# Attention with beacon keys and a squared-ReLU MLP: v of batches 0 and 1 cast in the transfer, chunk 1's second product by seven half-size products, second loads that wait for q, and a new order of work

## The chip, the cores and the metric

The kernel runs on one core of a Trainium2 chip. The metric is device time in microseconds (us) of one execution. Three runs of the kernel before took 327.59, 330.63 and 332.34 us, a median of 330.63. A core has TensorE (PE in the profile), VectorE (DVE), ScalarE (ACT), GpSimd (POOL) and SyncE (SP); DMA transfers are issued from the queues of SP, ACT and POOL, and only those that POOL issues change the data type on the way in this kernel.

## The reference

Eight batches, eight heads, 576 tokens, head size 64, and 16 "beacon" keys and values ahead of each head's own. Everything goes in and out in fp32.

```python
scores = matmul(q, concat([beacon_k, k]).T) / sqrt(64)      # causal over k; beacons are always seen
a = softmax(scores)
x = matmul(a, concat([beacon_v, v]))                        # -> x [4608 tokens, 512]
h = x @ w_in                                                # w_in  [512, 2048]
g = relu(h) ** 2
out = g @ w_out                                             # w_out [2048, 512]
```

## The kernel before

**Tiling.** Attention goes by batch and by pair of heads (four pairs p per batch, numbered on: batch b has pairs 4b to 4b+3). For a pair, scores are made with keys on the partitions (`qk` words, L695 in batch 0, L688 after it) into one of two PSUM strips, exponentiated by ACT into `pt` (`exp` words, L717 and L800), masked on the diagonal by a product with `tri` on DVE (`mask`, L823), multiplied with the 65-column tiles `vb` (v and a column of ones, so that the row sum comes along; `av`, L845), and normalised by DVE into `xn` (`norm`, L862 and L864). `xn` is transposed into `xT`, by TensorE in batches 0 to 2 (`xtp`, L913; evacuated by `xte` words on ACT or DVE) and by DMA from SP's queue after them (`xt`, L896).

The MLP goes by nine chunks j of 512 tokens. The first product is 16 groups of four 128x128x512 matmuls (`s1.j.f`, L1147), each evacuated through a relu (`relu`, ACT L1162 or DVE L1164) into `g` and squared in place, two groups at a time (`sq`, ACT L1172 or DVE L1174). Groups of chunk 0 are cut in a part 0 and a part 1, as batch 0 and batch 1 deliver its tokens. The second product has two forms. For j < FAST (chunks 0 and 1) it is plain: for each of four 128-token tiles, 16 matmuls 512 wide (`s2.j.ts.qd`, L1197) and one evacuation `ev`. For the other chunks it is done with seven products of half the size in place of eight: four sums of `g` in two parts on DVE (`sumj.n.i`, L1228), sums of `w_out` made once (`wsum`, L956), 14 groups of eight 256-wide matmuls (`s2.j.n.t`, L1256), and seven evacuations that add the products up in `osb` (`ev`, copies at L350 or L352 and adds at L1279). The first product of chunks 7 and 8 is also done with seven products (`h` words, L1024). A chunk's result goes out from `osb` by SP (`st`, L1185).

**Loads.** Batch 0's first part of q and k comes in fp32 into `osb` (`fldk`, `fldq`, L589: q of the first two pairs on ACT's queue, the others on SP's) and is cast by DVE or ACT (`fc`). Its second part (`sld0k1`, `sld0q1`) and batch 1's q and k (`sld1...`) come cast, by POOL's queue (L513), and are transposed by TensorE (`two`, `tp`, `ek`, `eq`). v comes by `add_load` in five tiles of up to 128 rows, eight heads and 64 columns: in batches 0 and 1 by POOL's queue, later by SP's, in fp32 into one of six slots `stg`, and from there a copy casts it into `vb` (`cast`, on POOL, at L352; two casts of batch 0 on DVE). `vb` has 65 columns per head, so a run of v in it is 128 bytes. `w_in` comes in four quarters by POOL's queue (`win0`, `win2`, `win1`, `win3`, L937), cast on the way, and so does `w_out` (`wout`, L945). From batch 2 on k comes by SP's queue into `stg` and q by POOL's (`ldq`), both are put into bf16 (`cast`, `join`) and transposed by DMA on SP (`tr`, L471).

**Order.** The list `SEQUENCE` is written out by hand: `Order.run` (L184) issues one operation for each word, in this order, so it fixes the order on every engine and every queue; a letter behind `@` picks the engine (A is ACT, D is DVE, P is POOL). Slots of `stg`, `ps` (four PSUM banks) and the strips are taken and given back in the same order. Where an operation has `sync`, each transfer that it issues waits for the transfer named there. `add_part_loads` has the parameter, and nothing gives it one.

## Time and profile before

| | before |
|---|---|
| three runs, us | 332.34, 327.59, 330.63 |
| profiled execution, us | 327.58 |
| its span, us | 325.8 |
| granted TensorE clock, mean | 0.998 |
| TensorE busy | 311.4 us, 96% |
| VectorE / ScalarE / GpSimd busy | 235.2 / 222.9 / 100.0 us |
| moved by DMA | 48.43 MB, mean 149 GB/s |

The span runs from the first to the last instruction of the profiled execution; the 1.8 us between it and that execution's time lie around it. TensorE has almost all of the span, so the questions are what its work takes, and where it waits. A row of a timeline has start, length, engine, line, operation, out<-in and count, and in brackets the idle time before it and what ended that. Letters and line numbers are those of the kernel before.

### The profile page before, as it was taken

The numbers are of one execution on the slowest core, as the hardware profiler recorded it, in microseconds if no ns is written. First come the engines' busy times: TensorE is split into PE (matmuls) and PEld (weight loads), VectorE is DVE, ScalarE is ACT, GpSimd is POOL, SyncE is SP. The second block draws the span as 40 slices with busy tenths as digits, with TensorE's granted clock in tenths as the row PEclk, the third lists the DMA queues.
The fourth block names the chain that finished last, engine by engine and source line by source line (L and its number), as shares of the span: only waits on it lengthen the run. The fifth ranks groups of instructions, "written<-read, shape, count | busy, mean of one in ns | idle before, by whom it ended". The sixth has DMA issues, their size and how long they took to land.

```text
span 325.8 us, 8454 instructions
## 1 busy us (share of the span) xinstructions
PE 311.4 (96%) x3440; PEld 226.1 (69%) x3460; DVE 235.2 (72%) x512; ACT 222.9 (68%) x333; POOL 100.0 (31%) x157
## 2 busy tenths in 40 slices
PE   2899899999999999999989999999999999999995
PEld 1579664644555468888776478655788788888884
DVE  3895985625545799666986687657968498989882
ACT  3996986378846897876755876648982664886810
POOL 9954852246610425240762114205000310000000
PEclk9999999999999999999999999999999999999999
DMA  7999999999994999898999995994500600030033
GB/s 156 213 204 210 201 206 174 175 181 258 200 161 115 224 222 179 126 193 168 262 152 164 199 221 139 178 206 117 127 14 9 179 19 2 0 132 0 2 147 113
DMA packets 127103, 48.43 MB, mean 149 GB/s; under 512 B 107864, under 2 KB 122072, under 8 KB 127064
## 3 DMA queue, kind: packets, MB, share of 16 engines
q1 hardware_dynamic: 108298, 35.48, 51.2%
q0 software_dynamic: 18112, 12.03, 25.3%
q8 instruction: 27, 0.44, 0.6%
q10 hardware_dynamic: 654, 0.38, 0.4%
q14 instruction: 12, 0.10, 0.1%
HBM read 37.22 MB, written 9.44 MB: 143 GB/s over the span
## 4 chain that ended last, share of the span: by engine, by line
PE 86%; DVE 5%; ACT 5%; DMA 1%; issue 1%; SPq 1%; ACTq 0%; DVEq 0%
PE ps L1147 27%; PE ps L1256 23%; PE ps L845 9%; PE ps L1197 8%; PE strip L1024 4%; PE strip L688 4%; PE ps L1024 3%; PE strip L1256 2%; PE ps L688 2%; PE strip L695 2%; DVE g L1174 2%; ACT pt L800 1%; DMA osb<-in_k_dram 1%; DVE pt L823 1%; PE ps L913 1%
## 5 line engine op out<-in xcount | busy, mean ns | idle before, releaser
L1147 PE MATMUL ps<-xT,w_in 128*128 128x512 bf16 (+6 forms) x626 | 103.4, 314 | 1.8 <-DVE g L1164 0.9
L1147 PEld LDWEIGHTS <-w_in 128*128 128x128 bf16 x640 | 57.4, 98 | 37.2 <-issue 2.9
L800 ACT ACTIVATE pt<-strip 128x1024 bf16<-128x1024 f32 (+3 forms) x77 | 70.4, 956 | 8.2 <-PE strip L688 4.6
L1162 ACT ACTIVATE g<-ps 128x512 bf16<-128x512 f32 (+2 forms) x80 | 42.4, 550 | 30.5 <-PE ps L1147 24.8
L1256 PEld LDWEIGHTS <-g 128*128 128x128 bf16 x448 | 42.5, 98 | 7.6 <-issue 1.9
L352 POOL CAST vb<-stg 128x512 bf16<-128x512 f32 (+1 forms) x38 | 25.9, 710 | 69.3 <-DMA stg<-in_v_dram 57.7
L823 DVE TENSOR_TENSOR pt<-pt,tri 128x512 bf16<-128x512 bf16 (+1 forms) x93 | 35.4, 404 | 13.2 <-ACT pt L800 12.9
L1164 DVE TENSOR_SCALAR g<-ps 128x512 bf16<-128x512 f32 (+2 forms) x48 | 29.0, 610 | 17.9 <-PE ps L1147 12.3
L845 PEld LDWEIGHTS <-pt 128*128 128x128 bf16 x930 | 34.8, 100 | 7.0 <-issue 0.9
L1256 PE MATMUL ps<-w_out,g 128*128 128x256 bf16 x304 | 38.3, 273 | 0.2 <-DVE xn L864 0.2
L845 PE MATMUL ps<-vb,pt 128*128 128x65 bf16 x930 | 37.4, 195 | 0.1
L1256 PEld LDWEIGHTS <-sum_area 128*128 128x128 bf16 x336 | 32.0, 98 | 5.4 <-issue 1.4
L864 DVE TENSOR_TENSOR xn<-ps,rcp 128x320 bf16<-128x320 f32 (+2 forms) x64 | 31.5, 492 | 2.2
L350 ACT COPY osb<-ps 128x512 f32<-128x512 f32 x24 | 14.0, 586 | 24.9 <-PE ps L1256 20.6
L352 POOL CAST qk_area<-stg 128x512 bf16<-128x512 f32 (+1 forms) x30 | 19.1, 657 | 38.3 <-DMA stg<-in_k_dram 38.0
L1172 ACT ACTIVATE g<-g 128x1024 bf16<-128x1024 bf16 (+2 forms) x32 | 29.6, 939 | 1.8 <-DVE g L1164 1.0
L1197 PE MATMUL ps<-w_out,g 128*128 128x512 bf16 x122 | 30.1, 379 | 0.3
L800 ACT ACTIVATE pt<-ps 128x512 bf16<-128x512 f32 x42 | 23.9, 601 | 8.8 <-PE ps L688 6.7
L1174 DVE TENSOR_TENSOR g<-g 128x1024 bf16<-128x1024 bf16 (+2 forms) x32 | 21.3, 681 | 9.3 <-ACT g L1162 9.2
L1256 PE MATMUL ps<-w_sum,sum_area 128*128 128x256 bf16 x208 | 27.0, 273 | 1.0 <-DVE osb L1279 1.0
L862 DVE RECIPROCAL rcp<-ps 128x5 f32<-128x5 f32 (+2 forms) x64 | 12.1, 189 | 12.8 <-PE ps L845 11.1
L688 PEld LDWEIGHTS <-kT 64*128 64x128 bf16 x432 | 13.9, 96 | 9.7 <-issue 7.4
(106 smaller groups left out, 407.5 us busy)
## 6 DMA issues: line engine op xcount, KB each, us to landing
out_dram<-osb SPq DMA_DIRECT2D x16, 512.0 KB, 3.4
stg<-in_k_dram SPq DMA_DIRECT2D x18, 256.0 KB, 4.5
stg<-in_v_dram SPq DMA_DIRECT2D x18, 256.0 KB, 4.9
stg<-in_q_dram POOLq DMA_DIRECT2D x12, 256.0 KB, 5.6
w_in<-in_moe_w_in_dram POOLq DMA_DIRECT2D x4, 512.0 KB, 11.7
w_out<-in_moe_w_out_dram POOLq DMA_DIRECT2D x4, 512.0 KB, 11.8
stg<-in_v_dram POOLq DMA_DIRECT2D x6, 256.0 KB, 8.6
stg<-in_k_dram SPq DMA_DIRECT2D x6, 224.0 KB, 4.3
```

What stands on the lines that cost most here:

```text
L352: eng[e].tensor_copy(dst, src)
L688: nc.tensor.matmul(out, kT[b % 2][hp, pr, 128 * c:128 * c + 128], rhs, start=True, stop=True)
L800: nc.scalar.activation(out, in_, AF.Exp, bias=0.0, scale=scale)
L823: nc.vector.tensor_tensor(out=d, in0=d, in1=tri[0:rows, m0:m0 + m, 0:w][:, None].to_broadcast([rows, 2, m, w]), op=ALU.min)
L845: nc.tensor.matmul(a[0:w, at + (t - tl[0]) * (D + 1):at + (t - tl[0] + 1) * (D + 1)], P[0:rr, hj, o:o + w], vb[b % 2][0:rr, c, 2 * pr + hj ...
L864: nc.vector.tensor_tensor(out=xn[b % 2].rearrange("p t (h d) -> p h t d", d=D)[:, h0:h0 + nh, tl[0]:tl[0] + nt], in0=a[:, :, :, 0:D], in1= ...
L1147: nc.tensor.matmul(h[:, lo - spans[0][0]:hi - spans[0][0]], w_in_sb[:, mc, ft * 128:(ft + 1) * 128], xT[:, mc, lo % RING:lo % RING + hi - lo],
L1162: nc.scalar.activation(dst, h, AF.Relu, bias=0.0, scale=1.0)
L1164: nc.vector.tensor_scalar(out=dst, in0=h, scalar1=0.0, scalar2=None, op0=ALU.max)
L1172: nc.scalar.activation(d, d, AF.Square, bias=0.0, scale=1.0)
L1197: nc.tensor.matmul(o, G[:, fc, ts * 128:(ts + 1) * 128], w_out_sb[:, fc, :], start=(fc == 0), stop=(fc == NFT - 1))
L1256: nc.tensor.matmul(o, lhs[:, f, t * 128:(t + 1) * 128], rhs[:, f], start=fresh and f == 0, stop=f == HF - 1, skip_group_check=True)
```

## The change

It has four parts.

1. v of batches 0 and 1 is written by the transfer straight into `vb` in bf16: no `stg` slot, no cast, the ten `cast0v` and `cast1v` words go. The transfers are on POOL's queue as before. Later batches' v is as before.
2. `FAST` goes from 2 to 1: chunk 1's second product is done by the seven half-size products. That adds eight `sum1` words and has 14 groups of eight for 16 of four, and seven evacuations for four.
3. The first transfer of batch 0's second part (`sld0k1.0`) waits for the transfer of the first q (`fldq0`).
4. `SEQUENCE` is written anew throughout: 1,532 words for 1,533, with the order changed in all batches and many engine letters too (relu on ACT 79 for 88, squares on ACT 48 for 43, joins on POOL fewer).

```diff
-    FAST = 2
+    FAST = 1
...
         soft = b <= 1
-        queue = nc.gpsimd if soft else nc.sync
+
+        if soft:
+            def emit_direct(e):
+                dst = vb[b % 2][:, c, :, 0:D]
+                insts = []
+                if lo:
+                    insts.append(nc.gpsimd.dma_start(out=dst[0:Nb], in_=beacon[b].transpose([1, 0, 2])))
+                insts.append(nc.gpsimd.dma_start(out=dst[lo:rows],
+                                                 in_=t[b, :, t0:t0 + rows - lo, :].transpose([1, 0, 2])))
+                return insts
+
+            ld = add(f"ld{b}{x}{c}", "POOL", 1.35 if lo else 0.9, emit_direct,
+                     dma=1.0 * rows / 128, behind=load_chain[-1:] + behind, sync=sync)
+            load_chain.append(ld)
+            cast[b, x, c] = ld
+            return
...
-        engs = ("POOL", "DVE") if b == 0 and c <= 1 else ("POOL",)
-        cast[b, x, c] = add(f"cast{b}{x}{c}", engs, {"DVE": 0.42, "POOL": 0.63}, emit_cast,
+        cast[b, x, c] = add(f"cast{b}{x}{c}", "POOL", 0.63, emit_cast,
                             deps=deps, give=ld)
...
         add("warm", "ACT", 1.5, emit_warm, behind=soons[-1:])
-        return first
+        return first, soons
...
-            first_loads = add_first_loads(add_beacon(0))
-            part_loads = add_part_loads(0, 1, [tri_op], [])
+            first_loads, soon_loads = add_first_loads(add_beacon(0))
+            part_loads = add_part_loads(0, 1, [tri_op], [], sync=soon_loads[:1])
```

The beginning of the new order, and the piece of it with chunk 1's second product:

```
ident bkl0 fldq0 fldq1 fldk0 tri warm fldk1 fldk2 fldq2 fldk3 bkc0 fldq3 fcq0@A sld0k1.0 tp0.0.0q fck0@A sld0q1.0
fcq1@D tp0.0.0k tp0.0.1q sld0k1.2 tpb0 fck1@D eq0.0.1@D ekb0 sld0q1.2 fck2@A bkl1 eq0.0.0@D tp0.0.2k ek0.0.0@D fcq2@A
ld0v0 ek0.0.2@A tpg0.0.0k tpg0.0.0q tp0.0.2q fck3@D tp0.0.1k tpg0.0.2k eq0.0.2@A ek0.0.1@D qk2.0.0 ld0v1 fcq3@D
...
relu1.12.0@A join3.2@P exp9.7.1.0.1 s2.1.1.0 ld3k3 join3.0@D joined3.1 relu1.8.0@A mask9.0.0 mask9.0.1 qk10.10
sq1.6.0@A mask9.0.2 sq1.4.0@D tr3q s2.1.1.1 exp10.10.-1.1.0 sum1.1.0 exp10.10.1.0.0 s2.1.2.0 sum1.1.1 ev1.c1.None@A
sum1.2.1 av9.0.0 exp10.10.0.0.0 s2.1.2.1 sum1.2.0 exp10.10.-1.0.0 norm9.0.0 cast3k2 s2.1.6.0 ld3k4 ev1.c11.None
cast3k3 qk11.13 mask10.0.0 ldq4.0 s2.1.5.0 sum1.3.1 exp11.13.-1.0.0 ldq4.1 mask10.0.1 exp11.13.-1.1.0 s2.1.6.1
mask10.0.2 sum1.4.0 ldq4.r sum1.3.0 av10.0.0 ev1.u2.None@A av9.0.1 cast3k1 exp11.13.0.0.0 s2.1.7.0 norm9.0.1 cast3k4
exp11.13.1.0.0 s2.1.5.1 mask11.0.0 tr3k norm10.0.0 s2.1.7.1 mask11.0.2 mask11.0.1 av10.0.1 join4.0@D ev1.u3.None@A
...
```

## The prediction

> **What bounds the kernel now.** I read the engine totals first, then busy time by stage, then what TensorE waited for. The page's head, and rows of the table by stage (start and end, length, then busy us of PE, PE's weight loads, DVE, ACT and POOL, the granted clock, DMA share, GB/s):

> ```profile
> span 325.8 us, 8454 instructions
> PE 311.4 (96%) x3440; PEld 226.1 (69%) x3460; DVE 235.2 (72%) x512; ACT 222.9 (68%) x333; POOL 100.0 (31%) x157
> ...
> 0.00:24.00 24.00, 16.87 (x231) 11.07 (x232) 16.64 (x58) 18.32 (x32) 19.17 (x35) 1.00 1.07 190
> 24.00:310.00 286.00, 282.43 (x3101) 204.39 (x3121) 210.10 (x439) 202.56 (x296) 80.82 (x123) 1.00 0.77 146
> 310.00:325.80 15.80, 12.10 (x111) 10.59 (x109) 8.44 (x17) 1.98 (x5) 0.00 (x0) 0.96 0.35 128
> ...
> 80.00:100.00 20.00, 19.78 (x221) 11.38 (x224) 10.70 (x31) 12.40 (x18) 7.71 (x11) 1.00 0.99 190
> 100.00:120.00 20.00, 19.78 (x180) 10.20 (x183) 14.93 (x31) 17.76 (x26) 6.09 (x10) 1.00 1.01 194
> ```

> TensorE is idle 14.4 us: 7.1 in the first 24 us, 3.6 in the next 286, 3.7 behind the last product. Between 24 and 310 us the kernel takes as long as its matmuls take, so fewer matmuls shorten it one for one, and a new wait lengthens it one for one. Who TensorE waited for (total, times, longest):

> ```profile
> PE ps L545 <- DVE qk_area L352: 5.4, 3, 4.6
> PE ps L1256 <- DVE osb L1279: 1.0, 1, 1.0
> PE ps L1147 <- DVE g L1164: 0.9, 1, 0.9
> ```

> The first is the start, before q and k arrive. The other two are the only waits of near 1 us behind it, and both come back below.

> **Chunk 1's second product.** Now it is 16 groups of four 512-wide matmuls; then 14 groups of eight 256-wide ones. From the chain that ended last (start, us), the two kinds of group, and from the timeline three pieces about chunk 3's sums, the same code that chunk 1 will run:

> ```profile
> 79.66 0.86 PE ps L1197 x4
> ...
> 120.11 0.87 PE ps L1256 x8
> ```

> ```profile
> 160.43 0.98 DVE L1228 TENSOR_TENSOR sum_area<-sum_area,g 128x1024 bf16<-128x1024 bf16 x1
> ...
> 160.88 1.00 POOL L352 CAST vb<-stg 128x512 bf16<-128x512 f32 x1
> ...
> 164.11 0.68 DVE L1228 TENSOR_TENSOR g<-g 128x1024 bf16<-128x1024 bf16 x1
> ```

> 16 x 0.86 = 13.8 becomes 14 x 0.87 = 12.2: **1.6 us less** on TensorE. Added: eight sums on DVE of 0.68 us alone, 0.98 beside a POOL cast, so 5.4 to 7.8 us, and seven evacuations for four, three of them on DVE. Over 80 to 120 us DVE has 25.6 of 40 us busy, so it holds them; the order of its work is the question. Product 6 needs both parts of sum 2. In the new order six groups stand between the last s1 group of chunk 1 and product 6, 5 us; the way through DVE is relu and square, then four sums, 0.7 + 0.8 + 4 x 0.68 to 0.98 = 4.2 to 5.4, behind masks. Two later casts of batch 3's k stand on POOL beside the sums. Seven chunks have this chain now, and only chunk 3 lost time in it (the 1.0 us above, where the sums ran beside casts). I take **0.7 us** of new wait, bounds 0 and 2 (twice the 1.0).

> **The v casts that go.** Ten casts leave POOL and DVE. Most of batch 1's, on POOL, stand here:

> ```profile
> 37.66 2.14 DVE L823 TENSOR_TENSOR pt<-pt,tri 128x512 bf16<-128x512 bf16 x1
> ...
> 38.13 0.84 POOL L352 COPY w_sum<-qk_area 96x768 bf16<-96x768 bf16 x1
> ...
> 38.90 1.93 POOL L352 CAST vb<-stg 128x512 bf16<-128x512 f32 x3
> ...
> 40.21 1.09 PE L1147 MATMUL ps<-xT,w_in 128*128 128x272 bf16 x8 [0.92 <-DVE g L1164]
> ```

> ```profile
> L823 DVE TENSOR_TENSOR pt<-pt,tri 128x512 bf16<-128x512 bf16 x62 | 28.3, 469 | 11.6 <-ACT pt L800 11.3
> ```

> A mask that takes 0.47 us in the mean took 2.14 while POOL copied and cast; the relu behind it was late and TensorE stood 0.92 us. Without the casts this goes: **-0.9 us** (bounds -0.9 and 0: two joins stay on POOL near there). [...]

> **The same loads by the transfer.** POOL's queue now, in the timeline, and transfers with their us from issue to landing (those issued at 6.86, about 10.2 and 12.32):

> ```profile
> 6.86 4.23 POOL L396 DMA_DIRECT2D stg<-in_v_dram  x5
> ...
> 12.32 0.77 POOL L937 DMA_DIRECT2D w_in<-in_moe_w_in_dram  x1 [0.26 <-DMA qk_area<-in_q_dram]
> ...
> 23.63 0.85 POOL L396 DMA_DIRECT2D stg<-in_v_dram  x1 [2.24 <-DMA w_in<-in_moe_w_in_dram]
> ```

> ```profile
> stg<-in_v_dram POOLq DMA_DIRECT2D x1, 224.0 KB, 6.6
> stg<-in_v_dram POOLq DMA_DIRECT2D x1, 160.0 KB, 7.9
> w_in<-in_moe_w_in_dram POOLq DMA_DIRECT2D x1, 512.0 KB, 11.0
> ```

> ```profile
> 9.00:14.00 5.00, 4.48 (x44) 2.67 (x43) 4.10 (x14) 4.80 (x11) 4.53 (x7) 1.00 1.26 227
> ...
> 18.20:28.50 10.30, 9.90 (x179) 8.31 (x179) 8.09 (x26) 8.83 (x18) 4.84 (x7) 1.00 1.25 206
> ```

> The queue is served in order and the transfer engines are full: v tiles land at 13.5 to 18.1, 1.15 us apart, and the second quarter of w_in at 23.3. POOL is held by its own older transfers (the idle 2.24 at 23.63 ends as that quarter lands), so taking the casts out of its way lets nothing land sooner. What a v tile costs when it is written as 128-byte runs in bf16 no row shows. By bytes written (206 GB/s while w_in is cast on the way, 227 while v isn't) it halves to 0.6 us; by runs it stays at 1.15; a run that is written badly may double it. I take 1.15, as runs of 1 KB and of 256 B move at nearly one rate here, so neither is cheap. Gain **0**: no matmul waits on v or w_in now.

> **Second loads wait for q.**

> ```profile
> 0.81 1.03 ACTq L589 DMA_DIRECT2D osb<-in_q_dram  x2
> ...
> 2.89 0.83 POOL L513 DMA_DIRECT2D qk_area<-in_k_dram  x1
> ...
> 8.02 0.41 ACT L350 CAST qk_area<-osb 120x256 bf16<-120x256 f32 x1 [1.34 <-DMA osb<-in_k_dram]
> 8.34 0.78 ACT L717 ACTIVATE pt<-strip 128x736 bf16<-128x736 f32 x1
> ...
> 22.90 1.05 ACT L717 ACTIVATE pt<-strip 128x928 bf16<-128x928 f32 x1
> ```

> ```profile
> osb<-in_q_dram ACTq DMA_DIRECT2D x2, 120.0 KB, 2.8
> ```

> POOL reaches its first load at 2.89; q's lands at 0.81 + 2.8 = 3.6. So **0.7 us** is put ahead of all that POOL issues behind it: part 1's other loads, v, w_in, batch 1's q, k and v, w_out, and batch 2's first loads, which wait for w_out (batch 2's q now right behind it on POOL, ahead of the memsets; nothing waits for it sooner). In exchange the first q and k run alone longer. That matters on ACT: it sat 1.34 us for the last k, with the first exponential ready behind it, and from 8.3 until the last exponential of batch 0 ends at 23.95 it has most of the 18.3 us that it works in the first 24. In the new order ACT casts q0 and k0 while it would be idle, the late cast is DVE's, and two evacuations of xT leave ACT. The best is 1.34 + 0.8 earlier; the worst is that w_in's second quarter, wanted first by s1.0.11.0, lands 0.7 later, at 24.0, where it is wanted at about 24.3. I take **-0.5**, bounds -2.1 and +1.

> **The new order.** All queues are rewritten, later batches too, and their covers shrink. Transfers' times from issue to landing, SP's issue of three xT transposes, a cast, attn x v of one head, and the score matmuls alone in their stage (30 visits, so 0.77 us of TensorE each):

> ```profile
> kT<-qk_area SPq DMA_TRANSPOSE x6, 5.0
> ...
> stg<-in_v_dram SPq DMA_DIRECT2D x6, 160.0 KB, 4.2
> ```

> ```profile
> 131.32 4.08 SPq L896 DMA_TRANSPOSE xT<-xn  x3
> ```

> ```profile
> L352 POOL CAST vb<-stg 80x512 bf16<-80x512 f32 x8 | 5.5, 693 | 3.0 <-PE ps L845 1.9 <-DMA stg<-in_v_dram 1.1
> ...
> 111.04 0.57 PE ps L845 x15
> ```

> ```profile
> 24.00:310.00 286.00, 23.05 (x432) 13.86 (x432) 1.00 0.77 146
> ```

> Batch 5's k transpose now has 25 TensorE groups between it and the scores that read it; then eight, five of 0.86 and three of 0.57, 6.0 us for a landing of 5.0. Batch 4's last v tile is issued behind the first xT transpose: 1.36 + 4.2 + 0.7 = 6.3 us to its cast, covered by five groups of 0.87 and two score visits, 5.9. What is late there is attn x v of pair 16, and all of TensorE behind it. So the 3.6 us of waits from 24 to 310 us don't shrink, and I add **1.0**, bounds -1.5 and +8 (some 1.5 us at each of five batches).

> **Sum.** The profiled execution took 327.58 us, 1.8 beside its span. 327.6 - 1.6 + 0.7 - 0.9 + 0 - 0.5 + 1.0 = **326.3** in its terms. It is level with the lowest of the runs shown (327.59, 330.63, 332.34), whose mean lies 2.6 above it; with that, **328.9** for a median.

> **Rivals.** *The 128-byte pieces are costly.* At twice the spacing five v tiles take 5.8 us more, w_in's second quarter lands at 23.3 + 0.7 + 5.8 = 29.8 instead of 24.3, and TensorE stands 5.5 us with s1.0.11.0 at its head: 326.3 + 5.5 + 2.6 = **334.4**, slower than before. It decides from a spacing of 1.2 us, so the margin is thin. For it: these are the shortest runs of the early queue. Against: the rates above hardly know the run length. [...]

> *The order runs just in time and misses.* Five batches lose 1.5 each: 7.5 instead of the 1.0 counted: 326.3 + 6.5 + 2.6 = **335.4**. For it: the two covers above. Against: the order now has been as full, at 98.8% from 24 to 310 us.

> *The start gives all it can.* -2.1 instead of -0.5, no wait in chunk 1 beyond 0.2, nothing lost to the order: 326.3 - 1.6 - 0.5 - 1.0 + 2.6 = **325.8**.

> *The products bring nothing*, as DVE gives back all 1.6 in chunk 1 (a wait of 1.6 for 0.7): **329.8**.

> **How the numbers follow.** Forecast 0.40, costly pieces 0.12, just in time 0.20, full start 0.18, products bring nothing 0.10. Two per cent, about what a measurement of this kernel tells from no change, is 324.0 and 337.2. Below 324.0 lies 0.11 (half of the full start, a little of the forecast), above 337.2 lies 0.20 (half of just in time, some of costly pieces, unseen waits), between them 0.69. The range 322.5 to 337.5 reaches past both slower cases; the likeliest case alone is 326 to 332.

> **What would show it.** Right: the group L1197 at half its count; no mask of 2 us near 38; the first exponential before 8.3; TensorE's waits from 24 to 310 us between 3 and 6 us in total. Wrong: v tiles landing over 1.2 us apart and w_in behind 24.3 with an idle TensorE; more than one wait over 1 us for kT, qT or vb in batches 3 to 7; waits for the sums over 2 us near 85 to 95.

## The result: 325.6 us for 331.4, a ratio of 0.989, and the profile after

The changed kernel took 324.55, 325.31, 325.84 and 331.09 us (median 325.57) beside 327.59 to 332.34 for the kernel before (median 331.4 of four). The ratio is **0.9891, 95% interval 0.9848 to 0.9934**: faster by about 1.1%, clear of the noise but within the two per cent that the prediction takes for what a measurement tells from no change. The forecast was 328.9 in a range of 322.5 to 337.5. The ratios here leave disturbed executions out, the medians count all. The profiled execution of after took 325.84 us, 1.7 less than that of before.

The page's head and the table by stage of after (start and end, length, then busy us of PE, PE's weight loads, DVE, ACT, POOL, granted clock, DMA share, GB/s):

```profile
span 324.1 us, 8555 instructions
PE 311.3 (96%) x3508; PEld 230.6 (71%) x3508; DVE 244.8 (76%) x538; ACT 221.4 (68%) x323; POOL 94.1 (29%) x142
...
0.00:24.00 24.00, 16.93 (x240) 11.08 (x241) 17.26 (x60) 17.61 (x28) 16.96 (x31) 1.00 1.49 169
24.00:310.00 286.00, 283.82 (x3182) 210.55 (x3179) 219.85 (x464) 202.65 (x292) 77.15 (x111) 1.00 0.83 145
310.00:324.10 14.10, 10.52 (x95) 9.01 (x93) 7.73 (x16) 1.12 (x3) 0.00 (x0) 1.00 0.33 120
```

TensorE's idle time is 7.1 us at the start (7.1 before), 2.2 in the middle (3.6 before) and 3.6 in the tail (3.7 before). Its busy time looks unchanged, 311.3 for 311.4, but the trace of before lacks 20 matmuls (3440 records for 3460 weight loads) and this one lacks none, so a saving in its work is hidden there, and some of the 3.6 us are gaps where only a record is missing: the waits of 0.2 us and more that the profile puts down to another engine in the middle come to 2.3 us in before and 2.0 in after. Whom TensorE waited for, and the plain second product, which is now at half its count (64 for 128, all records there):

```profile
PE ps L560 <- ACT qk_area L351: 4.0, 1, 4.0
PE ps L1271 <- DVE sum_area L1243: 1.6, 1, 1.6
...
PE ps L1271 <- DVE g L1243: 0.2, 1, 0.2
```

```profile
L1212 PE MATMUL ps<-w_out,g 128*128 128x512 bf16 x64 | 15.5, 379 | 0.0
```

The 1.0 us for `osb` in chunk 3 and the 0.9 us for a relu near 39 us are gone. Chunk 1's sums cost 0.2 us. New is 1.6 us in chunk 2. Its place in the timeline:

```profile
120.91 0.69 DVE L1243 TENSOR_TENSOR sum_area<-sum_area,g 128x1024 bf16<-128x1024 bf16 x1
...
121.52 2.05 DVE L838 TENSOR_TENSOR pt<-pt,tri 80x160 bf16<-80x160 bf16 x1
...
121.70 1.77 POOL L353 CAST vb<-stg 128x512 bf16<-128x512 f32 x3
...
123.49 0.68 DVE L1243 TENSOR_TENSOR sum_area<-sum_area,g 128x1024 bf16<-128x1024 bf16 x1
...
124.23 0.94 PE L1271 MATMUL ps<-w_sum,sum_area 128*128 128x256 bf16 x7 [1.56 <-DVE sum_area L1243]
```

A small mask (80x160, 0.35 us in the mean of 31) stood 2.05 us while GpSimd cast three tiles of batch 4's v, the sum behind it was late, and TensorE with it. It is the same kind of event as the one that the prediction read at 37.66 us of before, with other casts.

### The profile page after: what moved, and what is told of

Same layout as the page of the kernel before. It is cut to its first block, busy times and chain, and to the rows that moved or that the text cites. A ratio compares the mean times of both kernels' runs of the same rounds, so it can differ in the third digit from the quotient of the medians.

```text
span 324.1 us, 8555 instructions
## 1 busy us (share of the span) xinstructions
PE 311.3 (96%) x3508; PEld 230.6 (71%) x3508; DVE 244.8 (76%) x538; ACT 221.4 (68%) x323; POOL 94.1 (29%) x142
## 4 chain that ended last, share of the span: by engine, by line
PE 84%; DVE 6%; ACT 4%; DMA 3%; issue 1%; POOL 0%; DVEq 0%
PE ps L1162 27%; PE ps L1271 26%; PE ps L860 8%; PE ps L1212 4%; PE strip L1039 4%; PE strip L703 4%; PE ps L1039 3%; PE strip L1271 2%; DMA qk_area<-in_k_dram 2%; DVE sum_area L1243 2%; DVE pt L838 2%; PE strip L710 2%; PE ps L703 2%; ACT pt L815 1%; PE ps L928 1%
## 5 line engine op out<-in xcount | busy, mean ns | idle before, releaser
L1177 ACT ACTIVATE g<-ps 128x512 bf16<-128x512 f32 (+2 forms) x71 | 37.9, 555 | 27.7 <-PE ps L1162 27.0
L1271 PEld LDWEIGHTS <-g 128*128 128x128 bf16 x512 | 48.3, 98 | 8.3 <-issue 1.7
L1179 DVE TENSOR_SCALAR g<-ps 128x512 bf16<-128x512 f32 (+2 forms) x57 | 34.2, 612 | 18.4 <-PE ps L1162 17.1
L353 POOL CAST vb<-stg 128x512 bf16<-128x512 f32 (+1 forms) x30 | 22.3, 760 | 80.2 <-DMA stg<-in_v_dram 63.6
L1271 PE MATMUL ps<-w_out,g 128*128 128x256 bf16 x352 | 44.4, 273 | 0.2 <-DVE g L1243 0.2
L1271 PEld LDWEIGHTS <-sum_area 128*128 128x128 bf16 x384 | 36.3, 98 | 7.8 <-DVE sum_area L1243 2.2
L1187 ACT ACTIVATE g<-g 128x1024 bf16<-128x1024 bf16 (+2 forms) x38 | 35.2, 953 | 5.2 <-DVE g L1179 4.8
L1271 PE MATMUL ps<-w_sum,sum_area 128*128 128x256 bf16 x240 | 30.3, 273 | 1.6 <-DVE sum_area L1243 1.6
L1294 DVE TENSOR_TENSOR osb<-ps,osb 128x512 f32<-128x512 f32 (+1 forms) x26 | 16.8, 647 | 10.1 <-PE ps L1271 7.9
L1189 DVE TENSOR_TENSOR g<-g 128x1024 bf16<-128x1024 bf16 (+2 forms) x26 | 17.2, 674 | 6.4 <-ACT g L1177 6.2
L703 PEld LDWEIGHTS <-kT 64*128 64x128 bf16 x432 | 13.8, 96 | 8.9 <-issue 6.6
## 6 DMA issues: line engine op xcount, KB each, us to landing
out_dram<-osb SPq DMA_DIRECT2D x16, 512.0 KB, 4.2
w_in<-in_moe_w_in_dram POOLq DMA_DIRECT2D x4, 512.0 KB, 9.7
w_out<-in_moe_w_out_dram POOLq DMA_DIRECT2D x4, 512.0 KB, 10.5
stg<-in_k_dram SPq DMA_DIRECT2D x6, 224.0 KB, 4.6
stg<-in_v_dram SPq DMA_DIRECT2D x6, 224.0 KB, 3.3
```

Source lines behind the costliest of these rows:

```text
L353: eng[e].tensor_copy(dst, src)
L703: nc.tensor.matmul(out, kT[b % 2][hp, pr, 128 * c:128 * c + 128], rhs, start=True, stop=True)
L1177: nc.scalar.activation(dst, h, AF.Relu, bias=0.0, scale=1.0)
L1179: nc.vector.tensor_scalar(out=dst, in0=h, scalar1=0.0, scalar2=None, op0=ALU.max)
L1187: nc.scalar.activation(d, d, AF.Square, bias=0.0, scale=1.0)
L1271: nc.tensor.matmul(o, lhs[:, f, t * 128:(t + 1) * 128], rhs[:, f], start=fresh and f == 0, stop=f == HF - 1, skip_group_check=True)
```

## The experiments

Each kernel is named by what it starts from. For comparison, 74 executions of the kernel before stood beside these runs, with a median of 329.9 us.

| run | edit | median us (n) | ratio to before, 95% |
|---|---|---|---|
| a_again | changed kernel again | 325.45 (6) | 0.9885 (0.9825 to 0.9945) |
| b_look | kernel before again | 329.08 (1) | - |
| b_direct_v | before, v by the transfer | 329.12 (12) | 0.9984 (0.9940 to 1.0027) |
| b_c11_first | before, one order in chunk 3 | 328.91 (12) | 0.9959 (0.9919 to 0.9999) |
| b_prod1 | b_direct_v, products in chunk 1 | 334.22 (6) | 1.0153 (1.0116 to 1.0190) |
| a_no_wait | changed, no wait for q | 325.07 (6) | 0.9860 (0.9805 to 0.9915) |
| a_plain1 | changed, chunk 1 plain | 330.45 (12) | 1.0014 (0.9978 to 1.0050) |
| a_plain1_less | same, less weight sums | 328.14 (12) | 0.9972 (0.9940 to 1.0004) |
| a_more_sums | changed, two sums more | 328.61 (12) | 0.9972 (0.9943 to 1.0000) |
| a_sum_first | changed, one sum earlier | 325.20 (6) | 0.9869 (0.9827 to 0.9912) |
| a_direct_all | changed, all v by the transfer | 344.95 (6) | - |
| a_direct_late | same, v behind the transposes | 338.58 (6) | 1.0281 (1.0226 to 1.0336) |

**How large the difference is.** a_again has no edit.

> The changed kernel once more, beside the kernel before. Theory: the profile of after has its span 1.7 us under that of before, made of 1.6 less matmul work in chunk 1, 0.9 less where v's casts stood beside a mask, 1.0 less at chunk 3's sums, and a new wait of 1.6 at chunk 2's sums, so the difference is 1.5 to 2.5 us. Rival: the 330.6 of the median is the true level of the kernel before, and the difference is 3.5 to 5 us.

The ratio came out as before, and the medians differ by 4 to 6 us: the rival was nearer. The profiled execution of a_again took 323.71 us, 2.1 less than that of after with the same program, and 1.56 of it is chunk 2's wait, which it doesn't have; its longest wait behind the start is one for chunk 1's sums:

```profile
PE ps L1271 <- DVE g L1243: 0.4, 1, 0.4
```

So that meeting of a mask and casts is in one execution and not in the other of the same program. b_look is the kernel before, for a second trace.

> The kernel before once more, for its trace. Its runs so far spread from 327.6 to 337 us and the profiled one of before is the lowest. Theory: a usual execution has 3 to 4 us more of TensorE waiting than the 9.8 us of that trace, in several waits of 0.5 to 2 us behind VectorE, where VectorE's instruction stood beside a GpSimd cast or copy. Rival: the waits are the same, and TensorE's own work or the tail is longer.

It took 329.08 us and its trace is complete. Neither theory held: the waits from 24 to 310 us are 2.9 us, not 3 to 4 more, and the tail is the same. Two rows matter, TensorE's wait in chunk 3 and the plain product with all its records:

```profile
PE ps L1256 <- DVE osb L1279: 1.5, 1, 1.5
```

```profile
L1197 PE MATMUL ps<-w_out,g 128*128 128x512 bf16 x128 | 30.9, 379 | 0.0
```

The wait in chunk 3 is there again and longer (1.5 for 1.0). The one near 39 us is not: another draw. As neither this trace nor that of after lacks a matmul, they can be set side by side. This is the line of b_look's page:

```profile
PE 313.8 (96%) x3460; PEld 225.9 (69%) x3460; DVE 237.6 (73%) x512; ACT 222.9 (68%) x333; POOL 101.3 (31%) x157
```

TensorE's busy time is 313.8 us here and 311.3 in after, so 2.5 of the 3.1 us between the two spans (327.2 and 324.1) are its work. The product makes 1.6 of them; where the other 0.9 lies is not shown.

**Part 1 alone.** In the kernel before:

```diff
-        queue = nc.gpsimd if soft else nc.sync
+
+        if soft:
+            def emit_direct(e):
...
```

with the rest as in the change, and without the ten `cast0v` and `cast1v` words.

> The kernel before with part 1 of the change alone: v of batches 0 and 1 written into vb by the transfer, the ten casts gone, all else in the old order. Theory: the mask near 38 us takes 0.5 us instead of 2.1, TensorE's wait of 0.92 behind it goes, w_in's second quarter lands about 1.2 us earlier, and the time falls by 0.9 us. Rival A (128-byte pieces are costly): w_in's second quarter lands later than 24 us and the time rises by 1 to 5 us. Rival B (that wait has another cause): the mask stays long or the wait goes elsewhere, no change.

By medians 0.8 us under the 74 (2.3 under the 23 executions of before that ran beside it), by the ratio 0.5 with an interval from -2 to +0.9: the size that was expected, not shown apart from zero. Rival A is out: w_in's second quarter lands by 23.2 us, and nothing got slower. What TensorE waited for behind the start:

```profile
PE ps L1270 <- DVE osb L1293: 1.6, 1, 1.6
PE ps L702 <- DVE xn L878: 0.9, 1, 0.9
...
PE ps L1161 <- DVE g L1178: 0.6, 1, 0.6
```

The 0.6 is the place near 39 us. The mask takes 0.41 us there now, as the theory has it, but a VectorE copy of 1.04 us stood beside a GpSimd copy (both of them `two` words) and the wait is only a third shorter; the 0.9, at 229.8 us, stands behind three squares that took 3.44 us, from 225.66, partly beside three casts of later v.

**Chunk 3's wait.** The rows of before around it (the sums `sum3.4.1` and `sum3.3.0`, the evacuation `ev3.c11`, and TensorE):

```profile
161.45 0.98 DVE L1228 TENSOR_TENSOR sum_area<-g,sum_area 128x1024 bf16<-128x1024 bf16 x1
...
164.11 0.68 DVE L1228 TENSOR_TENSOR g<-g 128x1024 bf16<-128x1024 bf16 x1
...
164.72 0.68 DVE L1279 TENSOR_TENSOR osb<-ps,osb 128x512 f32<-128x512 f32 x1
...
165.45 1.03 PE L1256 MATMUL ps<-w_sum,sum_area 128*128 128x256 bf16 x8 [1.00 <-DVE osb L1279]
```

The edit, in the kernel before, to the words of VectorE's order:

```diff
 sum3.2.1
-sum3.4.1
 sum3.3.1
...
 mask20.0.1
-sum3.3.0
 ev3.c11.None
+sum3.3.0
+sum3.4.1
```

> The kernel before with one piece of VectorE's order changed in chunk 3: the evacuation that gives the PSUM bank back for product 5 stands ahead of two sums (sum3.3.0 and sum3.4.1), as the new order has it. Theory: the wait of 1.0 to 1.5 us near 165 us, which every trace in the old order shows and none in the new, is this order of VectorE's work; it goes, and the time falls by 1 to 1.5 us. Rival: the casts of v that stand beside the sums there make it, and the wait stays above 0.7 us.

The wait is gone from the trace while the casts stayed, so its cause is shown: the order of VectorE's work held a PSUM bank for two sums that nothing waited for yet. What it is worth is less sure. The ratio is 0.9959, 1.3 us, in an interval from 0.0 to 2.7. In the trace a part of the wait comes back three microseconds later, as one of the moved sums takes 1.53 us and the normalisations behind it are late:

```profile
166.24 1.53 DVE L1228 TENSOR_TENSOR sum_area<-g,sum_area 128x1024 bf16<-128x1024 bf16 x1
...
168.44 0.22 PE L688 MATMUL ps<-qT,kT 64*128 64x144 bf16 x1 [0.36 <-DVE xn L864]
169.07 0.34 PE L688 MATMUL ps<-qT,kT 64*128 64x144 bf16 x6 [0.41 <-DVE xn L864]
```

From the first group of the chunk's second product to the ninth it takes 11.8 us, for 11.7, 12.4 and 12.8 in the traces of before, b_look and b_direct_v. The new order has neither wait, in after, a_again and a_no_wait. The same trace has the meeting near 38 us in its worst form:

```profile
36.91 2.93 DVE L823 TENSOR_TENSOR pt<-pt,tri 128x512 bf16<-128x512 bf16 x1 [0.28 <-ACT pt L800]
...
37.84 2.48 POOL L352 CAST vb<-stg 128x512 bf16<-128x512 f32 x4
...
40.24 1.22 PE L1147 MATMUL ps<-xT,w_in 128*128 128x272 bf16 x8 [1.88 <-DVE g L1164]
```

The mask took 2.93 us beside four casts of batch 1's v, and TensorE waited 1.88. These are the casts that part 1 removes.

**Part 3 undone.**

```diff
-            part_loads = add_part_loads(0, 1, [tri_op], [], sync=soon_loads[:1])
+            part_loads = add_part_loads(0, 1, [tri_op], [])
```

> The changed kernel without part 3: the first second load does not wait for q. Theory: the second loads start at 2.9 instead of 3.9 us and land earlier, the first q and k land later by some tenths, first transpose by up to 0.5 us; the sum is within 0.4 us of the changed kernel. Rival: the wait is what starts the kernel earlier, and without it the time rises by 0.6 us or more.

325.07 for 325.45, level. The first exponential started at 8.38 us instead of 8.15, and a transposition of part 1 waited 1.4 us for VectorE: the loads did move, and it came to nothing.

```profile
2.88 0.83 POOL L528 DMA_DIRECT2D qk_area<-in_k_dram  x1
```

```profile
PE ps L560 <- DVE g L353: 1.4, 1, 1.4
```

**Part 2 undone, in three steps.** The first puts chunk 1's plain product in the places of the seven; the third and fourth weight sums must then stand behind it.

```diff
-    FAST = 1
+    FAST = 2
...
-wsum3
...
-wsum4
...
-s2.1.1.0
+s2.1.0.0
...
 mask12.0.1
+wsum3
...
 mask12.0.2
+wsum4
```

> The changed kernel with chunk 1's second product in the plain form again (16 groups in the places of the 14, four evacuations, no sums; the third and fourth weight sums behind it). Theory: TensorE gets 1.6 us of work back and loses the 0.2 us wait for the sums in chunk 1, so the time rises by 1.2 to 1.6 us. Rival: VectorE was giving the gain back elsewhere, and the time stays within 0.4 us.

It rose by 5.0 us, three times what the product is worth. The timeline shows why:

```profile
107.55 1.62 DVE L969 TENSOR_TENSOR w_out<-w_out 128x2048 bf16<-128x2048 bf16 x1
...
109.83 1.02 PE L1160 MATMUL ps<-xT,w_in 128*128 128x512 bf16 x4 [0.54 <-DVE g L1177]
...
111.00 1.21 DVE L969 TENSOR_TENSOR w_sum<-w_out,w_sum 128x2048 bf16<-128x2048 bf16 x1
...
112.87 1.02 PE L1160 MATMUL ps<-xT,w_in 128*128 128x512 bf16 x3 [1.24 <-DVE g L1177]
```

The weight sums delay relus, and TensorE waits behind each, 1.8 us together. The second step gives the changed kernel two sums more at that place.

```diff
+            add(f"more{i}", "DVE", 1.25, lambda e: nc.vector.tensor_tensor(
+                out=w_sum[4], in0=w21, in1=w_sum[2], op=ALU.subtract), deps=prev)
```

> The changed kernel with the fourth weight sum made twice more on VectorE at the place where the plain form of chunk 1 leaves the third and fourth (behind the first masks of batch 3), 2 x 1.22 us of added VectorE work. Theory: that place is full, relus and squares of chunk 2 come late, and the time rises by 2 to 3.5 us; then the early weight sums are a part of what FAST = 1 brings. Rival: VectorE has room there, the time stays within 0.7 us, and the 5 us of the plain form in the new order were its own.

3.2 us more: in the new order the place is full. In the order of before the same two sums stand at 104 to 107 us, between relus of chunk 2 as well, and cost nothing there:

```profile
104.21 1.22 DVE L956 TENSOR_TENSOR w_out<-w_out 128x2048 bf16<-128x2048 bf16 x1
...
106.30 1.22 DVE L956 TENSOR_TENSOR w_sum<-w_out,w_sum 128x2048 bf16<-128x2048 bf16 x1
```

From 80 to 150 us none of the four traces with this order (before, b_look, b_direct_v, b_c11_first) has a wait of TensorE of 0.2 us or more. The third step takes the plain form without that load.

```diff
-  (3, w12, w22, w12, (2, 3)), (4, w_sum[4], w21, w_sum[2], (2, 3))):
+  (4, w_sum[4], w21, w_sum[2], (2, 3))):
```

with `wsum4` at its early place again.

> The changed kernel with chunk 1's second product plain again, as in the earlier run (330.4 us median), but without the third weight sum at all (left out: product 7 then takes the weights unsummed, so the output differs from the reference) and with the fourth at its early place of the changed kernel. Theory: the 5 us of that run were 1.6 for the product and some 3 for the two weight sums at a full place of VectorE, so this one lies 1 to 2 us above the changed kernel, 326.3 to 327.4. Rival: the plain form's own evacuations and bank waits cost 3 us or more in the new order, 328.5 or above.

2.7 us above a_again, between the theory and the rival. TensorE's busy time is 313.2 us, 1.9 more than in after, both traces complete. Of its waits, two are not in the changed kernel's trace without the meeting in chunk 2:

```profile
PE ps L1270 <- DVE sum_area L1242: 1.1, 1, 1.1
...
PE ps L1211 <- DVE osb L351: 0.5, 1, 0.5
```

The 1.1 is not the plain form's: it stands at chunk 2's sums, beside three casts of batch 4's v, and a_more_sums, which has chunk 1 in seven products, has the same 1.1 at the same place. The 0.5 is: it is a wait for a bank of the plain product, and a_plain1 has it too. So the product is worth 1.6 to 1.9 us of work and 0.5 us of waits, and what is left of the 2.7 is within the noise. FAST = 1 also lets the weight sums stand early, at 65 to 69 us. That is worth up to 3 us in the new order; it is no gain over the kernel before, where they cost nothing.

**Products in the old order.**

```diff
-    FAST = 2
+    FAST = 1
...
+wsum3
 sq1.2.0@D
...
+wsum4
 sq1.1.0@D
...
-s2.1.2.0
+s2.1.1.0
...
 sq1.6.0@A
+sum1.1.0 sum1.1.1 sum1.2.1 sum1.2.0
```

> The kernel before with v by the transfer (part 1) and chunk 1's second product by seven products (part 2), all else in the old order; the third and fourth weight sums stand at 65 to 70 us on VectorE instead of 104 to 107. Theory: against the run with part 1 alone (329.1 us median) 1.6 us of TensorE's work goes, and what the weight sums delayed near 105 to 125 us goes with it, so 1.6 to 4 us less, 325 to 327.5. Rival: the new order is what brings the rest, and without it this stays at 328 or above, as VectorE gives back what TensorE saves.

5 us slower than b_direct_v: the rival is right, though neither it nor the theory has the size. Its waits are a mask (0.7 us), squares (1.2) and evacuations (0.9) in chunk 1's stretch and a mask behind it (1.0). Behind the first two the granted clock was 0.50 for 3.4 us (last section). The places were chosen by hand, so it shows that the product does not pay at these places; what the best places in the old order would give is not shown.

**A way to a better version.** First the sum ahead of the mask that stood 2.05 us.

```diff
 ev2.c1.None@A
+sum2.2.0
 mask15.0.2
 av13.0.0
-sum2.2.0
```

> The changed kernel with one sum of chunk 2 (sum2.2.0) ahead of the mask of pair 15 that took 2.05 us beside a GpSimd cast in the trace of after. Theory: that wait of 1.56 us stood in one trace of three of the changed kernel; with the sum ahead the wait for the sums stays under 0.5 us, and the median falls by 0.2 to 0.8 us. Rival: the sum itself then takes 2 us beside the cast, or the mask makes attention of pair 15 late: no gain.

The wait is absent, as it is in a_again without this edit, and 325.20 is within the noise of 325.45: no better version is shown. Then v of all batches by the transfer, which takes the last thirty casts away:

```diff
-        soft = b <= 1
+        soft = x == "v"
```

> The changed kernel with v of all batches written into vb by the transfer on GpSimd's queue: the thirty casts of v that are left (22.3 us of GpSimd) go, thirty loads (about 0.75 us of GpSimd each) come to its queue from SyncE's. Theory: VectorE instructions beside these casts no longer take up to 2 us, chunk 2's wait for its sums (1.56 us in one trace of after) can't come back, and the median falls by 0.5 to 2 us with less spread. Rival: the loads stand behind GpSimd's other work and its queue, v of batches 3 to 6 lands late, and the time rises by 1 us or more.

20 us slower. VectorE's long instructions are mostly gone, as expected (of those with two inputs five are over 0.3 us above the median of their line and shape, 2.1 us in all, for 14 and 7.4 us in after), but in the trace, which is of the slowest of the six executions, TensorE waits for k:

```profile
PE strip L701 <- DMA kT<-qk_area: 17.9, 3, 9.1
```

```profile
kT<-qk_area SPq DMA_TRANSPOSE x6, 11.4
```

The transposes of k took 11.4 us from issue to landing in the median, for 5.5 in after. TensorE's busy time is 317.8 us for 311.3 as well, at a mean granted clock of 0.97. In after SyncE issues v at 65.5 us, behind k's transpose of 61.8; here GpSimd issues it from 59.8 to 64.0 us, and SyncE the transpose at 63.5, while a transfer of v lands as late as 67.5. The next run has it wait:

```diff
                 behind = trans[b, "q"] + trans[b, "k"]
+                sync = trans[b, "k"]
```

> The changed kernel with v of all batches by the transfer on GpSimd's queue, but with the first v load of batches 2 to 7 waiting for the landing of that batch's k transpose. Theory: the 17.9 us of waits for kT in the run without this wait came from v's transfers beside the transposes (a k transpose of batch 2 took 15.6 us from issue to landing); with them apart the waits for kT fall under 2 us, VectorE's long instructions beside the casts stay away, and the median is between 1.5 us below and 1 us above the changed kernel. Rival: 128-byte pieces on GpSimd's queue are the trouble, wherever they stand, or GpSimd's waiting holds up k's casts and the next q: 5 us or more above the changed kernel.

The waits for k went (its transposes took 5.3 us), so they came from v's transfers beside them. But the time stayed 13 us high, as the rival has it. GpSimd does nothing from 59.0 to 68.0 us, until k's transpose has landed; behind that come v's loads and then, at 72.7 us (69.4 in after), those of the next q. VectorE's joins wait for q, and the masks stand behind the joins:

```profile
83.79 0.29 DVE L351 COPY qk_area<-stg 128x512 bf16<-128x512 bf16 x1 [6.91 <-DMA stg<-in_q_dram]
...
84.61 0.56 DVE L836 TENSOR_TENSOR pt<-pt,tri 128x512 bf16<-128x512 bf16 x2
85.08 1.02 PE L858 MATMUL ps<-vb,pt 128*128 128x65 bf16 x15 [5.64 <-DVE pt L836]
```

Elsewhere TensorE waited 3.0 us for v itself and 2.7 for an evacuation. How much of this is GpSimd's waiting and how much the 128-byte pieces beside q's transfer is not told apart.

## Why the prediction was right, and where it was not

The direction was right, the time lies in the range, and 3.3 us under the forecast. The range was 15 us wide for a change of 3.6, and of the terms only the product's work came out as forecast. That the sum of 326.3, ahead of its last step, lies 0.7 us from the median is in part luck: the start's -0.5, the order's +1.0 and the casts' -0.9 are not borne out singly and come to -0.4 together. Step by step:

- **Chunk 1's product, -1.6 + 0.7.** The work is right (64 wide matmuls fewer, 0.22 us each, 112 half-size ones more, 0.11 each). The wait was 0.2 and 0.4 us in two traces, not 0.7. The sum leaves out that the weight sums move ahead of chunk 2, and rightly: where they stood in before they cost nothing.
- **Casts, -0.9.** Without the casts the mask there took 0.41 us (b_direct_v) for 2.14 in before, but the row it was read from was one draw. Why a mask is long beside a cast no run shows. At that place TensorE lost 0.92 us in the trace of before, 1.88 in b_c11_first and nothing in b_look, and after has the same kind of meeting at 121.5 us with casts that stay. The gain is a mean over draws, 0.5 to 0.8 us by b_direct_v, with an interval across zero. The bound of 0 was set for copies that stay on GpSimd near there, and in b_direct_v one of them met VectorE.
- **v by the transfer, 0.** Right in effect. The rows of after:

```profile
3.87 0.83 POOL L528 DMA_DIRECT2D qk_area<-in_k_dram  x1 [0.94 <-DMA osb<-in_q_dram]
...
7.30 4.33 POOL L397 DMA_DIRECT2D vb<-in_v_dram  x5
...
22.23 0.83 POOL L397 DMA_DIRECT2D vb<-in_v_dram  x1 [1.69 <-DMA w_in<-in_moe_w_in_dram]
```

  GpSimd starts a microsecond later, and yet w_in's second quarter lands by 22.2 us instead of 23.6. That is not the tiles alone: it is 23.0 in b_look, with v through `stg`, and 23.2 in b_direct_v. The tiles land 0.9 to 1.0 us apart (13.8 to 17.6 us in after), a little cheaper than the 1.15 taken, so the rival of costly pieces falls for this stage. Its doubled spacing was a supposition of the author's; no run shows it.
- **Start, -0.5.** It gave nothing: 7.1 us idle in the first 24 both times, and a_no_wait is level. The rival "the start gives all it can" has the right number, 325.8, by a wrong way.
- **Order, +1.0.** The wrong sign. None of the feared waits for kT, qT or vb came in batches 3 to 7, and chunk 3's wait went, 0.0 to 2.7 us by b_c11_first. The prediction named that wait and then laid it to casts beside the sums; it quoted sums but not the evacuation behind them, so the order did not show in its rows. It also took all 3.6 us of idling from 24 to 310 us for waits, of which about 1 us is missing records, and expected 3 to 6 us there; after has 2.2.
- **+2.6 from the profiled execution to the median.** The largest miss. For before it holds: the profiled execution was the fastest of the first four, only six of the 74 are faster, and their median lies 2.3 above it. It was then carried over to the changed kernel, whose profiled executions lie 0.3 above (325.84) and 1.7 below (323.71) the medians of their runs. That the distance is made of meetings of VectorE and GpSimd, which the change lessens, is argued and not shown.

The parts measured alone (-2.7 for the product in the new order, -1.3 for chunk 3, -0.5 for v) add up to -4.5, against -3.6 by the ratio. Each is uncertain by 1 to 2 us either way, so this does not contradict the whole, nor prove it. How the rest of the new order contributes can't be told from these runs.

## What to carry to other kernels

One trace is one draw: the wait near 40 us was 0.92 us in before, 1.88 in b_c11_first and absent in b_look, so look at a second trace before its size goes into a sum, and don't carry the distance between a lucky profile and the median over to the changed kernel. In a hand-written order, look for instructions that stand ahead of the one that gives a buffer back and that nobody waits for yet; moving two such sums took a wait of 1.0 to 1.6 us away, and some of it came back behind what they then stood ahead of. When a load moves to another queue, look for what it stood behind in the old one: v of the later batches, moved from behind k's transposes on SyncE's queue to GpSimd's, cost 20 us (a_direct_all), and 13 us were left when a wait gave that order back (a_direct_late).

## What the runs showed of the hardware

**Behind about 1.9 us of idling within 3.41 us the clock was 0.50 for the next 3.41.** The table by stage of b_c11_first around its wait of 1.88 us, and of b_prod1 around its waits of 0.73 and 1.18 us (the columns as above; the granted clock stands behind POOL):

```profile
37.65:41.07 3.42, 1.54 (x14) 1.10 (x13) 3.37 (x4) 2.44 (x4) 3.37 (x7) 1.00 1.24 197
41.07:44.48 3.41, 3.41 (x23) 2.59 (x21) 1.64 (x5) 1.01 (x2) 2.86 (x5) 0.50 1.24 208
44.48:47.89 3.41, 3.41 (x61) 2.42 (x60) 2.63 (x9) 3.40 (x7) 0.00 (x0) 1.00 1.26 204
```

```profile
86.55:89.96 3.41, 1.50 (x21) 1.11 (x20) 1.86 (x4) 3.30 (x5) 2.34 (x3) 1.00 1.18 137
89.96:93.37 3.41, 3.41 (x23) 1.96 (x21) 3.34 (x9) 0.64 (x2) 0.00 (x0) 0.50 1.22 192
```

In b_c11_first the matmuls from 37.73 to 44.87 us take 7.1 us, the same ones in b_look 3.8: 1.9 us more are the wait and 1.5 work at the lower clock, so that wait cost nearly twice its length. Behind after's wait of 1.56 us the clock stays at 1.00:

```profile
124.30:126.00 1.70, 1.70 (x27) 1.57 (x28) 1.49 (x5) 0.00 (x0) 0.00 (x0) 1.00 1.56 189
```

By these numbers one stretch of 3.41 us at 0.50 lowers the mean over a span of 327 us by 0.005. It fits that 19 of the 74 executions of the kernel before had a mean granted clock of 0.995 or less (330.4 to 337.4 us) and one of ten of the changed kernel (331.09). That the casts near 38 us made those is not shown, as none of these was profiled. Of twelve executions each, b_direct_v, without these casts, has one such mean and b_c11_first, with them, four; but b_prod1, without them, has three of six, and its trace lost the clock at 90 us.

**v in 128-byte pieces took more of the transfer engines' time.** The queues of after and of a_direct_all (packets, MB, share of 16 engines; q0 is GpSimd's):

```profile
q0 software_dynamic: 26944, 10.82, 31.7%
```

```profile
q0 software_dynamic: 55936, 14.46, 52.3%
```

From after to a_direct_all q0 takes 182 us of the engines' time instead of 103, while the other queue falls from 53.0% to 42.5%, 172 to 148 us. Thirty tiles of v cost 80 us as bf16 pieces of 128 bytes and 24 us as fp32 on SyncE's queue. In batches 0 and 1 there is a rise as well: from before to b_direct_v, with the same ten tiles on the same queue, q0 rises from 25.3% to 33.1% of the span, 82 to 109 us. Yet there the tiles landed no later (0.9 to 1.0 us apart in after, 1.15 in before), and b_direct_v was no slower (329.12 us for 329.9).
